# The opening stage of a pooled-attention and feed-forward kernel: keys of batch 1 loaded and pooled earlier, units of the first projection in another order

## The chip, the core and the metric

The kernel runs on one core of a Trainium2 chip. The metric is the time of one execution on the device in microseconds (us). TensorE (PE) multiplies, VectorE (DVE) and ScalarE (ACT) read its results out of PSUM, GpSimd (POOL) works between buffers in SBUF and also issues loads through its own software queue, and SyncE (SP) issues loads, stores and transposing transfers through a hardware queue. Each engine runs its instructions in the order of the program and waits on semaphores for the others.

## The reference, cut to what matters

```python
q, k, v: (8, 8, 576, 64) float32          # batch, heads, sequence, head size
k_p = k.reshape(B, H, 72, 8, D).mean(axis=3)   # 8 neighbouring keys become one
v_p = v.reshape(B, H, 72, 8, D).mean(axis=3)
scores = q @ k_p.T / sqrt(D);  attn = softmax(scores)
x = (attn @ v_p) as (4608, 512)
h = x @ w_in                               # w_in  512 x 2048
g = h - tanh(h)
out = g @ w_out                            # w_out 2048 x 512
```

## The kernel before, in words

Each of the 8 batches gives 512 queries to a group of its own (g = 0 to 7), in four blocks of 128 queries (j = 0 to 3). The 64 queries left over in each batch, its tail, are collected in pairs of batches and form a ninth group. For a group the kernel computes scores, softmax and attention for each block, turns the result x into xT, multiplies it with w_in (w1b in SBUF) to h, forms g = h - tanh(h) in gT, and multiplies with w_out (w2b). While one group is in its two large products, the attention of the next group is slipped in between.

The order of all work is written out by hand, and each engine gets its instructions in that order. PSUM has eight banks of 512 columns, and each use of a bank names its number.

The change lies in the opening stage, group 0, where nothing can be slipped under large products yet. These parts are touched:

* **Loads on the queue of POOL.** `load_w1(c)` (L187) brings the quarter c of w_in, the four quarters of hidden units, and casts it to bf16 on the way; `load_w2(c)` (L192) does so for w_out. `load_rows` (L131 and L137, two transfers) brings keys or values of a batch, `load_q` (L141) its queries. The order on this queue is: values of batch 0, w1 quarters 0, 1, 2, keys of batch 1, w1 quarter 3, queries of batch 1, w2 quarter 0, values of batch 1, w2 quarters 1 and 2, and later, behind other work of POOL, w2 quarter 3, queries of batch 2 and the tail of batches 0 and 1 (`tail_pieces`, L171).
* **Pooling keys.** `pool_k(1, nc.gpsimd)` adds eight keys to one in three additions on POOL (L209, L212, L215) and leaves them in kd. PE turns kd in five small products (`k_turn_pe`, recorded under L273), and DVE places the result in KB (L247).
* **Casting and turning queries.** `q_cast` (L261) makes bf16 from float32, one block each; `q_turn_pe` lets PE turn a block in four small products and ACT copy it into qT (L670).
* **h units.** `h_mm_quad(c, j, bank)` (L446) computes a quarter c of the hidden units, four times 128, for the block j: 16 products into one bank. It needs w1's quarter c and xT of the block j. `h_act_quads(c, j, bank)` (L472 tanh on ACT, L473 subtraction on DVE) empties two banks that hold the quarter c of the blocks j and j + 1. `h_tanh_quad` (L458) and `h_sub_quad` (L462) empty a single bank. xT of the blocks 2 and 3 comes last: `x_turn_pe` turns it on PE, and ACT copies it (L418).

There are 16 units (c, j). Behind them stands the second product of group 0, in 16 steps `o_unit0(u)` of four products each (L483): steps 0 to 3 use w2's quarter 0, steps 4 to 7 its quarter 1, and so on. Between these steps stand the scores (`s_unit`, L292 on PE, L304 and L307 on DVE), exponentials and values of batch 1. Step 1 releases the keys of batch 2, issued by SP (L131, L137); DVE pools them behind step 10, and SP turns them.

The tile framework gives the transfers of each kind of queue eight semaphores in rotation, so an issue waits until the transfer eight before it in the same rotation has landed.

Of the kernel before, what the change touches and what calls it, by code (L numbers as in the profile page):

```python
# [8 lines left out]
FP32 = mybir.dt.float32  # L9
BF16 = mybir.dt.bfloat16  # L10
ACT = mybir.ActivationFunctionType
# [9 lines left out]
R = 4  # L21
# [4 lines left out]
TG = 512  # L26
# [12 lines left out]
def kernel(  # L39
# [9 lines left out]
    nc = tc.nc  # L49
# [5 lines left out]
    tpool = ctx.enter_context(tc.tile_pool(name="tpool", bufs=3))  # L55
    psum = ctx.enter_context(tc.tile_pool(name="psum", bufs=1, space=PSUM))
    PS = psum.tile([128, 8, 512], FP32, name="PS")
    ctx.enter_context(tc.manual_schedule())

    def flat(b0, n):  # L60
        return PS[:, b0 : b0 + 2, :].rearrange("p k c -> p (k c)")[:, 0:n]
# [14 lines left out]
    gT = const.tile([128, NHID, TG], BF16, name="gT")  # L76
# [5 lines left out]
    q_raw = [const.tile([128, H, R, D], FP32, name=f"q_raw{i}") for i in range(2)]  # L82
# [42 lines left out]
    def load_rows(src, dst, b, t0=0, t1=NT, eng=None):  # L125
        eng = eng or nc.sync
        r = []
        n1 = min(t1, 4)
        if t0 < n1:
            r.append(  # L130
                eng.dma_start(  # L131
                    out=dst[:, t0:n1, :],
                    in_=src[b, 128 * t0 : 128 * n1, :].rearrange("(t p) n -> p t n", p=128),
                )
            )
        if t1 == NT:
            r.append(eng.dma_start(out=dst[0:64, 4, :], in_=src[b, 512:NK, :]))  # L137
        return r

    def load_q(b, dst, j0=0, j1=R, eng=None):  # L140
        return (eng or nc.sync).dma_start(  # L141
            out=dst[:, :, j0:j1, :],
            in_=q[b, :, 0:QA, :].rearrange("h (p j) d -> p h j d", j=R)[:, :, j0:j1, :],
        )
# [5 lines left out]
    def k_pieces(b):  # L150
        return row_pieces(k_rows, k_raw, b)
# [13 lines left out]
    def run(pieces, n=16):  # L165
        for _ in range(min(n, len(pieces))):
            pieces.pop(0)()

    def tail_pieces(i, eng=None):
        return [  # L170
            lambda s=s: (eng or nc.sync).dma_start(  # L171
                out=tl_raw[64 * s : 64 * s + 64, :, :],
                in_=q[2 * i + s, :, QA:S, :].rearrange("h p d -> p h d"),
            )
            for s in range(2)
        ]
# [9 lines left out]
    def load_w1(c):  # L186
        return nc.gpsimd.dma_start(  # L187
            out=w1b[:, :, c * 512 : (c + 1) * 512], in_=w1_src[:, :, c * 512 : (c + 1) * 512]
        )

    def load_w2(c):
        return nc.gpsimd.dma_start(  # L192
            out=w2b[:, c * 4 : (c + 1) * 4, :], in_=w2_src[:, c * 4 : (c + 1) * 4, :]
        )
# [10 lines left out]
    def pool_k(b, eng, t0=0, t1=NT):  # L205
        r = k_raw[b % 2].rearrange("p t (j d) -> p t j d", d=D)[:, t0:t1, :, :]
        kd = kds[b % 2][:, t0:t1, :, :]
        n = t1 - t0
        eng.tensor_tensor(  # L209
            out=r[:, :, 0:4, :], in0=r[:, :, 0:4, :], in1=r[:, :, 4:8, :], op=ALU.add  # L210
        )
        eng.tensor_tensor(  # L212
            out=r[:, :, 0:2, :], in0=r[:, :, 0:2, :], in1=r[:, :, 2:4, :], op=ALU.add
        )
        return eng.tensor_tensor(  # L215
            out=kd,
            in0=r[:, :, 0:1, :].to_broadcast([128, n, 2, D]),
            in1=r[:, :, 1:2, :].to_broadcast([128, n, 2, D]),
            op=ALU.add,
        )  # L220
# [39 lines left out]
    def q_cast(b, eng, j0=0, j1=R):  # L260
        eng(  # L261
            out=q_bf[b % 2][:, j0:j1, :, :].rearrange("p j h d -> p h j d"),
            in_=q_raw[b % 2][:, :, j0:j1, :],
        )
# [177 lines left out]
    def h_mm_quad(c, j, bank):  # L442

        for n in range(4):
            for fb in range(NFB):
                mm = nc.tensor.matmul(  # L446
                    PS[:, bank, 128 * n : 128 * n + 128],
                    lhsT=w1b[:, fb, (4 * c + n) * 128 : (4 * c + n + 1) * 128],
                    rhs=xT_of(0)[:, j, fb, :],
                    start=(fb == 0),  # L450
                    stop=(fb == NFB - 1),
                    skip_group_check=True,
                )
        return mm

    def h_tanh_quad(bank):
        t_sb = tpool.tile([128, 2, TG], FP32, name="t_sb2", tag="t_sb2")[:, 0, :]
        nc.scalar.activation(out=t_sb, in_=PS[:, bank, :], func=ACT.Tanh)  # L458
        return t_sb

    def h_sub_quad(c, j, bank, t_sb):
        nc.vector.tensor_sub(  # L462
            out=gT[:, 4 * c : 4 * c + 4, 128 * j : 128 * j + 128],
            in0=PS[:, bank, :].rearrange("p (n c) -> p n c", n=4),
            in1=t_sb.rearrange("p (n c) -> p n c", n=4),
        )

    def h_act_quads(c, j, bank):

        ps = PS[:, bank : bank + 2, :]  # L470
        t_sb = tpool.tile([128, 2, TG], FP32, name="t_sb2", tag="t_sb2")
        nc.scalar.activation(out=t_sb[:, :, :], in_=ps, func=ACT.Tanh)  # L472
        nc.vector.tensor_sub(  # L473
            out=gT[:, 4 * c : 4 * c + 4, 128 * j : 128 * j + 256].rearrange(
                "p n (j c) -> p j n c", j=2
            ),
            in0=ps.rearrange("p j (n c) -> p j n c", n=4),
            in1=t_sb.rearrange("p j (n c) -> p j n c", n=4),
        )
# [141 lines left out]
    ve, se, ge = nc.vector.tensor_copy, nc.scalar.copy, nc.gpsimd.tensor_copy  # L621
# [19 lines left out]
    for base, sign in ((G, 1), (-1, -1)):  # L641
        nc.gpsimd.affine_select(
            out=mask[:, :, :, 0],
# [20 lines left out]
    def q_turn_pe(b, j, bank, eng):  # L664
        for m in range(NHP):
            turn(
                PS[:, bank, m * 128 : (m + 1) * 128],
                q_bf[b % 2][:, j, 2 * m : 2 * m + 2, :].rearrange("p h d -> p (h d)"),
            )
        eng(out=qTs[b][:, j, :, :].rearrange("p m c -> p (m c)"), in_=PS[:, bank, :])  # L670
# [19 lines left out]
    w1_dmas.append(load_w1(1))  # L690
    for j in range(2, 4):
        q_cast(0, ge, j, j + 1)
    w1_dmas.append(load_w1(2))
    after(w1_dmas[1:], pooled)
    load_rows(k_rows, k_raw[1], 1, eng=nc.gpsimd)
    load_w1(3)
    load_q(1, q_raw[1], eng=nc.gpsimd)
    load_w2(0)
    load_rows(v_rows, v_bf[1], 1, eng=nc.gpsimd)
    load_w2(1)  # L700
    load_w2(2)
    kps = flat(4, NT * 128)
    k_turn_pe(0, 0, 2, kps)
    fill(1, 7)
# [48 lines left out]
    normalise((0, 1), x0[3])  # L753
    h_sub_quad(0, 1, 6, h_tanh_quad(6))
    h_sub_quad(1, 1, 7, h_tanh_quad(7))
    h_mm_quad(2, 0, 4)
    h_mm_quad(2, 1, 5)
    x_turn_pe(x0[3], 0, 3, 3, se)
    h_act_quads(2, 0, 4)
    pool_k(1, nc.gpsimd)  # L760
    load_w2(3)
    for j in range(R):
        q_cast(1, ge, j, j + 1)
    load_q(2, q_raw[0], eng=nc.gpsimd)
    run(tail_pieces(0, nc.gpsimd))
    h_mm_quad(0, 2, 6)
    h_mm_quad(0, 3, 7)
    h_act_quads(0, 2, 6)
    h_mm_quad(1, 2, 2)
    h_mm_quad(1, 3, 3)  # L770
    h_act_quads(1, 2, 2)
    h_mm_quad(2, 2, 4)
    kps = flat(0, NT * 128)
    k_turn_pe(1, 0, NT, kps)
# [1 line left out]
    h_mm_quad(2, 3, 5)  # L776
    h_act_quads(2, 2, 4)
    h_mm_quad(3, 0, 6)
    q_turn_pe(1, 0, 0, se)
    h_mm_quad(3, 1, 7)  # L780
    h_act_quads(3, 0, 6)
    q_turn_pe(1, 1, 1, se)
    h_mm_quad(3, 2, 2)
    h_sub_quad(3, 2, 2, h_tanh_quad(2))
    q_turn_pe(1, 2, 0, se)
    h_mm_quad(3, 3, 3)
    h_sub_quad(3, 3, 3, h_tanh_quad(3))
    q_turn_pe(1, 3, 1, se)

    def load_for(g):  # L790
# [41 lines left out]
    for u in range(16):  # L832
        mm = o_unit0(u)
        if u == 1:
            after(load_rows(k_rows, k_raw[0], 2, 0, 2), mm)
            run(k_pieces(2)[1:])
        if u == 0:
            exp_unit(0, s_unit(0, PA))
        if u == 1:
            exp_unit(1, s_unit(1, PB))  # L840
        if u == 2:
            sh2 = s_unit(2, PA)
        if u == 3:
            v_unit(2)
            exp_unit(2, sh2)
        if u == 4:
            e_turn_pe(slot(4), 0, se)
            exp_unit(3, s_unit(3, PB))
        if u == 5:
            e_turn_pe(slot(5), 0, se)  # L850
        if u == 6:
            e_turn_pe(slot(6), 2, se)
        if u == 7:
            a_unit(0, PA)
            e_turn_pe(slot(7), 2, se)
        if u == 8:
            a_unit(1, PA)
            x_turn_dma(x1[0], 1, 0, 2)
        if u == 9:
            a_unit(2, PB)  # L860
        if u == 10:
            a_unit(3, PA)
            x_turn_dma(x1[1], 1, 2, 2)
            for t in range(0, NT, 2):
                pool_k(2, nc.vector, t, min(t + 2, NT))
            q_turn_dma(2)
            k_turn_dma(2)
            k_place_kT(2, ge)
            run(v_pieces(2))
            turn_tail(0)  # L870
            load_for(1)
        if u >= 12:
            o_store(0, u % 4, OB[u % 4], (se, ve)[u % 2])
# [208 lines left out]
```

## Time and profile before

| | |
|---|---|
| median of 3 runs | 300.4 us (300.05 to 300.6) |
| the profiled execution, whole | 301.8 us |
| its span, first to last instruction | 300.1 us |
| mean granted TensorE clock | 0.991 |
| busy share of the span: PE, DVE, ACT, POOL | 95%, 69%, 48%, 41% |
| chain that ended last, by engine: PE, DVE, DMA | 77%, 8%, 7% |

The sums of the prediction are made against the profiled execution, which is 1.4 us above the median of the runs. In the rows of a timeline the first number is the start in us from the start of the span, the second the time in which the group of instructions was busy; brackets at the end give how long the engine sat idle before it, and what released it. A row "DMA to landing" gives smallest, median and largest time from the issue of a transfer to its landing. In the rows of a table by stretches each engine has its busy time and, in brackets, its instructions; PEclk is the granted clock of TensorE.

### The profile page before, as it was taken

The numbers are of one execution on the slowest core, as the hardware profiler recorded it, in microseconds if no ns is written. First come the engines' busy times: TensorE is split into PE (matmuls) and PEld (weight loads), VectorE is DVE, ScalarE is ACT, GpSimd is POOL, SyncE is SP. The second block draws the span as 40 slices with busy tenths as digits, with TensorE's granted clock in tenths as the row PEclk, the third lists the DMA queues.
The fourth block names the chain that finished last, engine by engine and source line by source line (L and its number), as shares of the span: only waits on it lengthen the run. The fifth ranks groups of instructions, "written<-read, shape, count | busy, mean of one in ns | idle before, by whom it ended". The sixth has DMA issues, their size and how long they took to land.

```text
span 300.1 us, 5150 instructions
## 1 busy us (share of the span) xinstructions
PE 286.5 (95%) x2011; PEld 167.5 (56%) x2027; DVE 206.2 (69%) x292; ACT 142.9 (48%) x200; POOL 121.7 (41%) x111
## 2 busy tenths in 40 slices
PE   6799799999999999999999999999999999999993
PEld 2489765444554455445544554455447854784582
DVE  6786484878835993398339932986699947945772
ACT  1786255158504851476137623672376345505620
POOL 7846906029610791098107910791063830010000
PEclk9999799999999999999999999999999999999998
DMA  7999996699988999886889798959823540011005
GB/s 233 225 283 272 205 264 172 129 262 314 228 219 212 332 151 217 239 298 114 204 248 312 137 185 257 328 73 214 232 68 69 103 167 17 2 70 73 0 3 140
DMA packets 84377, 54.55 MB, mean 182 GB/s; under 512 B 58976, under 2 KB 72416, under 8 KB 84352
## 3 DMA queue, kind: packets, MB, share of 16 engines
q1 hardware_dynamic: 77552, 44.90, 57.8%
q0 software_dynamic: 6416, 8.91, 14.3%
q10 hardware_dynamic: 384, 0.39, 0.5%
q8 instruction: 16, 0.26, 0.4%
q14 instruction: 9, 0.07, 0.1%
HBM read 36.70 MB, written 9.44 MB: 154 GB/s over the span
## 4 chain that ended last, share of the span: by engine, by line
PE 77%; DVE 8%; DMA 7%; POOL 3%; ACT 2%; issue 1%; SPq 0%; ACTq 0%; POOLq 0%; DVEq 0%
PE PS L426 32%; PE PS L483 26%; PE PS L561 11%; DMA k_raw<-in_k_dram 4%; PE PS L379 4%; DVE gT L440 3%; DMA q_raw<-in_q_dram 3%; PE PS L292 2%; DVE sh L307 2%; DVE mx L304 2%; PE PS L446 1%; POOL k_raw L209 1%; ACT t_sb L439 1%; PE PS L273 1%; POOL k_raw L212 1%
## 5 line engine op out<-in xcount | busy, mean ns | idle before, releaser
L440 DVE TENSOR_TENSOR gT<-PS,t_sb 128x1024 bf16<-128x1024 f32 x64 | 77.0, 1219 | 40.2 <-ACT t_sb L439 40.2
L426 PE MATMUL PS<-xT,w1b 128*128 128x512 bf16 x448 | 100.8, 379 | 0.0
L483 PE MATMUL PS<-w2b,gT 128*128 128x512 bf16 x368 | 88.7, 379 | 0.8
L439 ACT ACTIVATE t_sb<-PS 128x1024 f32<-128x1024 f32 x64 | 65.5, 1024 | 48.4 <-PE PS L426 47.0
L426 PEld LDWEIGHTS <-w1b 128*128 128x128 bf16 x512 | 49.4, 98 | 55.8
L483 PEld LDWEIGHTS <-gT 128*128 128x128 bf16 x384 | 35.3, 98 | 36.8
L505 ACT COPY o_h<-PS 128x512 f32<-128x512 f32 x22 | 12.8, 583 | 47.7 <-PE PS L483 44.0
L224 POOL TENSOR_TENSOR v_raw<-v_raw 128x1280 f32<-128x1280 f32 x6 | 17.4, 2908 | 35.7 <-DMA v_raw<-in_v_dram 35.7
L343 ACT ACTIVATE E<-sh 128x576 bf16<-128x576 f32 x31 | 21.2, 682 | 15.9 <-DVE sh L307 15.9
L307 DVE TENSOR_TENSOR sh<-PS,mx 128x576 f32<-128x576 f32 x35 | 26.5, 757 | 1.2
L304 DVE TENSOR_REDUCE mx<-PS 128x8 f32<-128x576 f32 x35 | 26.2, 748 | 1.5 <-PE PS L292 1.5
L400 DVE RECIPROCAL rden<-PS 128x8 f32<-128x8 f32 x36 | 7.4, 205 | 25.4 <-PE PS L379 23.4
L401 DVE TENSOR_TENSOR x_sb<-PS,rden 128x512 bf16<-128x512 f32 x32 | 22.1, 692 | 1.1
L561 PEld LDWEIGHTS <-q_raw 128*128 128x128 bf16 x192 | 18.5, 98 | 2.9 <-DVE q_raw L543 0.4
L247 POOL COPY KB<-kT 64x288 bf16<-64x288 bf16 x12 | 5.1, 421 | 35.6 <-DMA kT<-kd 30.2
L209 POOL TENSOR_TENSOR k_raw<-k_raw 128x1280 f32<-128x1280 f32 x6 | 17.4, 2908 | 0.0
L446 PE MATMUL PS<-xT,w1b 128*128 128x128 bf16 x256 | 17.2, 230 | 0.0
L446 PEld LDWEIGHTS <-w1b 128*128 128x128 bf16 x256 | 16.2, 104 | 0.0
L379 PEld LDWEIGHTS <-ET 128*128 128x128 bf16 x192 | 13.1, 98 | 5.2 <-ACT ET L362 0.8
L379 PE MATMUL PS<-VB,ET 128*128 128x130 bf16 (+2 forms) x192 | 15.8, 221 | 0.1
L561 PEld LDWEIGHTS <-gT 128*128 128x128 bf16 x144 | 13.9, 98 | 2.0
L292 PEld LDWEIGHTS <-qT 128*128 128x128 bf16 x128 | 10.0, 98 | 7.6 <-issue 0.8
(99 smaller groups left out, 290.7 us busy)
## 6 DMA issues: line engine op xcount, KB each, us to landing
k_raw<-in_k_dram SPq DMA_DIRECT2D x14, 512.0 KB, 8.6
q_raw<-in_q_dram SPq DMA_DIRECT2D x12, 512.0 KB, 6.9
v_raw<-in_v_dram SPq DMA_DIRECT2D x12, 512.0 KB, 5.1
out_dram<-o_h SPq DMA_DIRECT2D x24, 256.0 KB, 2.5
w1b<-in_moe_w_in_dram POOLq DMA_DIRECT2D x4, 512.0 KB, 9.0
q_raw<-in_q_dram POOLq DMA_DIRECT2D x2, 1024.0 KB, 14.2
w2b<-in_moe_w_out_dram POOLq DMA_DIRECT2D x4, 512.0 KB, 16.4
out_dram<-o_h SPq DMA_DIRECT2D x4, 512.0 KB, 3.3
```

The source lines that it names most:

```text
L209: eng.tensor_tensor(out=r[:, :, 0:4, :], in0=r[:, :, 0:4, :], in1=r[:, :, 4:8, :], op=ALU.add)
L304: nc.vector.reduce_max(out=mx.rearrange("p k h o -> p k (h o)"), in_=sc, axis=AX.X)
L307: nc.vector.tensor_tensor(out=sh[:, :, :, :], in0=sc, in1=mx.to_broadcast([128, 2, 4, G]), op=ALU.subtract)
L343: nc.scalar.activation(out=E[:, e, :, :].rearrange("p t c -> p (t c)")[:, 0:NK], in_=sh.rearrange("p k h c -> p (k h c)"), func=ACT.Exp, s ...
L379: nc.tensor.matmul(PS[ps, banks[half], D1 * h : D1 * (h + s1 - s0)], lhsT=ET[:, t, c0 : c0 + (ps.stop - ps.start)], rhs=VB[kb][:, t, s0:s1 ...
L401: nc.vector.tensor_tensor(out=x_sb, in0=ps[:, :, :, 0:D], in1=rden.to_broadcast([128, 2, 4, D]), op=ALU.mult,)
L426: nc.tensor.matmul(PS[:, bank, :].rearrange("p (j c) -> p j c", j=R), lhsT=w1b[:, fb, i * 128 : (i + 1) * 128], rhs=xT_of(g)[:, :, fb, :], ...
L439: nc.scalar.activation(out=t_sb[:, :, :], in_=ps, func=ACT.Tanh)
L440: nc.vector.tensor_sub(out=gT[:, i : i + 2, :], in0=ps, in1=t_sb[:, :, :])
L446: mm = nc.tensor.matmul(PS[:, bank, 128 * n : 128 * n + 128], lhsT=w1b[:, fb, (4 * c + n) * 128 : (4 * c + n + 1) * 128], rhs=xT_of(0)[:, ...
L483: mm = nc.tensor.matmul(PS[:, bank, 0 : c1 - c0], lhsT=gT[:, i, tb * 128 : (tb + 1) * 128], rhs=w2b[:, i, c0:c1], start=(i == 0), stop=(i ...
L561: nc.tensor.matmul(ps, lhsT=A[:, i, 128 * b : 128 * b + 128], rhs=B_[:, i, :], start=(n in "24" and i == 0), stop=(i == NQ - 1), skip_grou ...
```

## The change

On the queue of POOL the keys of batch 1 move ahead of w1's quarter 2. `pool_k(1)` moves from behind the first h units to the place ahead of the issues of w2's quarters 1 to 3; the casts of the queries of batch 1, w2's quarter 3 and the queries of batch 2 follow there in a row. The tail of batches 0 and 1 is no longer issued by POOL but by SP, at step 1 of the second product, behind the keys of batch 2. The h units come in another order: the blocks 2 and 3 of the quarters 0 and 1 first, then quarter 2. The units of one block and two quarters are emptied together by the new `h_act_quads2`. The turns of the queries of batch 1 stand one h unit later each, and the last two stand together.

```diff
+    def h_act_quads2(c, j, bank):
+        ps = PS[:, bank : bank + 2, :]
+        t_sb = tpool.tile([128, 2, TG], FP32, name="t_sb2", tag="t_sb2")
+        nc.scalar.activation(out=t_sb[:, :, :], in_=ps, func=ACT.Tanh)
+        nc.vector.tensor_sub(
+            out=gT[:, 4 * c : 4 * c + 8, 128 * j : 128 * j + 128],
+            in0=ps.rearrange("p k (n c) -> p (k n) c", n=4),
+            in1=t_sb.rearrange("p k (n c) -> p (k n) c", n=4),
+        )
...
     w1_dmas.append(load_w1(1))
     for j in range(2, 4):
         q_cast(0, ge, j, j + 1)
-    w1_dmas.append(load_w1(2))
     after(w1_dmas[1:], pooled)
     load_rows(k_rows, k_raw[1], 1, eng=nc.gpsimd)
+    load_w1(2)
     load_w1(3)
     load_q(1, q_raw[1], eng=nc.gpsimd)
     load_w2(0)
     load_rows(v_rows, v_bf[1], 1, eng=nc.gpsimd)
+    pool_k(1, nc.gpsimd)
     load_w2(1)
     load_w2(2)
+    for j in range(R):
+        q_cast(1, ge, j, j + 1)
+    load_w2(3)
+    load_q(2, q_raw[0], eng=nc.gpsimd)
...
-    h_mm_quad(2, 0, 4)
-    h_mm_quad(2, 1, 5)
+    h_mm_quad(0, 2, 4)
     x_turn_pe(x0[3], 0, 3, 3, se)
-    h_act_quads(2, 0, 4)
-    pool_k(1, nc.gpsimd)
-    load_w2(3)
-    for j in range(R):
-        q_cast(1, ge, j, j + 1)
-    load_q(2, q_raw[0], eng=nc.gpsimd)
-    run(tail_pieces(0, nc.gpsimd))
-    h_mm_quad(0, 2, 6)
-    h_mm_quad(0, 3, 7)
-    h_act_quads(0, 2, 6)
-    h_mm_quad(1, 2, 2)
-    h_mm_quad(1, 3, 3)
-    h_act_quads(1, 2, 2)
+    h_mm_quad(1, 2, 5)
+    h_act_quads2(0, 2, 4)
+    h_mm_quad(0, 3, 6)
+    h_mm_quad(1, 3, 7)
+    h_act_quads2(0, 3, 6)
+    h_mm_quad(2, 0, 2)
+    h_mm_quad(2, 1, 3)
+    h_act_quads(2, 0, 2)
     h_mm_quad(2, 2, 4)
     kps = flat(0, NT * 128)
     k_turn_pe(1, 0, NT, kps)
     k_place(1, kps[:, 0:NK], (ve, ve))
     h_mm_quad(2, 3, 5)
     h_act_quads(2, 2, 4)
     h_mm_quad(3, 0, 6)
-    q_turn_pe(1, 0, 0, se)
     h_mm_quad(3, 1, 7)
     h_act_quads(3, 0, 6)
-    q_turn_pe(1, 1, 1, se)
+    q_turn_pe(1, 0, 0, se)
     h_mm_quad(3, 2, 2)
     h_sub_quad(3, 2, 2, h_tanh_quad(2))
-    q_turn_pe(1, 2, 0, se)
+    q_turn_pe(1, 1, 1, se)
     h_mm_quad(3, 3, 3)
     h_sub_quad(3, 3, 3, h_tanh_quad(3))
+    q_turn_pe(1, 2, 0, se)
     q_turn_pe(1, 3, 1, se)
...
         if u == 1:
             after(load_rows(k_rows, k_raw[0], 2, 0, 2), mm)
             run(k_pieces(2)[1:])
+            run(tail_pieces(0))
```

## The prediction

> **What bounds the kernel now.** I read the page first, for the engine that fills the span and for places where it doesn't.
>
> ```profile
> span 300.1 us, 5150 instructions
> PE 286.5 (95%) x2011; PEld 167.5 (56%) x2027; DVE 206.2 (69%) x292; ACT 142.9 (48%) x200; POOL 121.7 (41%) x111
> PEclk9999799999999999999999999999999999999998
> ```
>
> PE is busy for 95%, so time is won only where PE stands still or runs slowly. The clock row shows one such place: the fifth slice (30.0 to 37.5 us). The table by stretches of 2 us shows it closer.
>
> ```profile
> 30.00:32.00 2.00, 0.01 (x1) 0.02 (x2) 1.23 (x1) 0.00 (x0) 1.92 (x3) 1.00 1.25 207
> 32.00:34.00 2.00, 2.00 (x20) 2.00 (x21) 0.91 (x2) 0.00 (x0) 2.00 (x4) 0.52 1.23 203
> 34.00:36.00 2.00, 2.00 (x26) 2.00 (x24) 0.56 (x1) 1.02 (x1) 2.00 (x4) 0.63 1.24 206
> ```
>
> The first engine column is PE: 0.01 us of work from 30 to 32 us, then granted clocks of 0.52 and 0.63. The chain of waits, cut to the first 64 us, names the cause.
>
> ```profile
> 12.24 12.50 DMA k_raw<-in_k_dram
> ...
> 25.03 0.74 POOL w2b L192
> ...
> 25.78 2.92 POOL k_raw L209
> ...
> 30.41 1.53 POOL kd L215
> 31.98 0.66 PE PS L273 x5
> 32.64 3.21 PE PS L446 x32
> ```
>
> The keys of batch 1 are issued at 12.24 and land at 24.74; POOL pools them from 25.78 until 31.94, 6.16 us; PE turns them at 31.98. PE's own timeline shows what it does around this.
>
> ```profile
> 23.13 1.95 PE L446 MATMUL PS<-xT,w1b 128*128 128x128 bf16 x32
> 24.91 0.39 PE L273 MATMUL PS<-ident,x_sb 128*128 128x128 bf16 x4
> 25.14 4.63 PE L446 MATMUL PS<-xT,w1b 128*128 128x128 bf16 x80
> 31.98 0.66 PE L273 MATMUL PS<-ident,kd 128*128 128x128 bf16 x5 [2.22 <-POOL kd L215]
> 32.43 3.42 PE L446 MATMUL PS<-xT,w1b 128*128 128x128 bf16 x32
> 35.69 0.39 PE L273 MATMUL PS<-ident,q_bf 128*128 128x128 bf16 x4
> ...
> 39.26 1.03 PE L483 MATMUL PS<-w2b,gT 128*128 128x512 bf16 x3
> ...
> 45.11 1.03 PE L483 MATMUL PS<-w2b,gT 128*128 128x512 bf16 x4
> ...
> 58.52 6.21 PE L426 MATMUL PS<-xT,w1b 128*128 128x512 bf16 x28
> ```
>
> At full clock 32 products take 24.91 - 23.13 = 1.78 us, 0.056 each, so a unit of 16 takes 0.89. The 80 products from 25.14 thus issue until 29.6: PE stands for 2.4 us. The next 32 take 35.69 - 32.43 = 3.26, which is 1.48 too long, and the five turns 0.45 for 0.28: another 0.17. **The stall costs 2.4, the low clock behind it 1.65, together 4.05 us.**
>
> **The change, part by part.** *Keys ahead of w1's quarter 2.* POOL's rows show when transfers land, since its issues wait for earlier ones.
>
> ```profile
> 18.24 0.54 POOL L137 DMA_DIRECT2D v_raw<-in_v_dram  x1 [1.52 <-DMA w1b<-in_moe_w_in_dram]
> 20.80 0.76 POOL L192 DMA_DIRECT2D w2b<-in_moe_w_out_dram  x1 [2.02 <-DMA w1b<-in_moe_w_in_dram]
> ...
> 31.87 0.78 POOL L192 DMA_DIRECT2D w2b<-in_moe_w_out_dram  x1
> 32.65 2.27 POOL L261 CAST q_bf<-q_raw 128x512 bf16<-128x512 f32 x4
> 34.87 0.90 POOL L141 DMA_DIRECT2D q_raw<-in_q_dram  x1
> 35.76 1.40 POOL L171 DMA_DIRECT2D tl_raw<-in_q_dram  x2
> ```
>
> POOL goes on 0.3 us after a landing (keys at 24.74, issue at 25.03). So w1's quarter 1 landed at about 18.0, quarter 2 at 20.5, 2.5 later, and the keys another 4.2 later. If the queue stays first in, first out, the keys land 2.5 (a quarter's time) to 4.2 us (their own) behind 18.0: at 20.5 to 22.2, and their fifth piece, issued 0.7 later, at most 0.4 behind. I take 22.5, by their own row. POOL starts 0.3 later, and kd is ready at 22.8 + 6.2 = 29.0 (bounds 27.0 and 29.1; before 31.94). The three transfers that swap have the same bytes, so w1's quarter 2 lands by 25.1 and its quarter 3 about when it did.
>
> *The order of the h units.* The timelines of ACT and DVE give what PE has to wait for.
>
> ```profile
> 22.97 0.58 ACT L418 CAST xT<-PS 128x512 bf16<-128x512 f32 x1 [0.42 <-PE PS L273]
> ...
> 28.97 1.02 ACT L472 ACTIVATE t_sb<-PS 128x1024 f32<-128x1024 f32 x1 [0.82 <-PE PS L446]
> ...
> 39.89 0.63 ACT L670 CAST qT<-PS 128x512 bf16<-128x512 f32 x1
> ```
>
> ```profile
> 26.88 2.52 DVE L473 TENSOR_TENSOR gT<-PS,t_sb 128x1024 bf16<-128x1024 f32 x2 [1.36 <-ACT t_sb L472]
> ...
> 32.57 0.94 DVE L247 CAST KB<-PS 64x288 bf16<-64x288 f32 x2 [1.32 <-PE PS L273]
> ...
> 55.25 0.68 DVE L209 TENSOR_TENSOR k_raw<-k_raw 128x512 f32<-128x512 f32 x1
> ```
>
> At 23.13 PE now wants xT of block 2 and finds it when ACT's copy ends, 22.97 + 0.58: a new wait of 0.4 us. From 23.5 it has 7 units (6.2) and a turn of x (0.2) before the turn of the keys, and comes to it at 29.95, where kd lies ready for 1.0 us (0.9 to 2.9 by the bounds). The 2.4 us go, and the low clock with them.
>
> Banks: a pair of units is emptied by 1.02 (tanh), 1.26 (subtraction, half of 2.52) and 0.3 for handovers (tanh at 28.97, behind products that end at 25.14 + 64 x 0.056 = 28.7), so 2.6 us behind its last product. By that the pairs are empty at 28.1, 29.9 and 31.6, and PE wants the banks again at 29.1, 31.1 and 33.1; w1's quarter 2 is wanted at 27.3, quarter 3 at 31.1. DVE places the keys behind the third subtraction, from 31.6 until 32.5, and the first turn of the queries wants that bank at 32.9: 0.4 to spare, the tightest cover; without it PE would wait one for one.
>
> *The turns of the queries.* The last ACT work ahead of the scores is four copies of about 0.5 and two single tanh of about 0.5 behind the pair's tanh. The pair ends on PE at 32.9, its tanh at 34.1, and the six run in a row until 37.15; before, the last copy ended at 39.89 + 0.63 = 40.5, and the scores of batch 1 wait for its bank. PE waits 0.3 for a bank ahead of the fourth turn, since two turns now stand together, and starts the second product at 35.9 instead of 39.26. Both differences are 3.35.
>
> **The sum:** -2.4 (stall) -1.65 (clock) +0.4 (xT of block 2) +0.3 (bank of the fourth turn) = -3.35 us at the scores of batch 1.
>
> *Loads behind the pooling.* w2's quarter 1 was issued at 20.80 and now waits for the pooling, until 29.0. Its landing, and that of the quarter issued at 31.87, by line:
>
> ```profile
> L192 POOL DMA_DIRECT2D w2b<-in_moe_w_out_dram x1: 764/764/764, 20.8 to 20.8; - x1
> ...
> DMA to landing us min/median/max: 17.2/17.2/17.2
> ```
>
> ```profile
> L192 POOL DMA_DIRECT2D w2b<-in_moe_w_out_dram x1: 780/780/780, 31.9 to 31.9; - x1
> ...
> DMA to landing us min/median/max: 11.3/11.3/11.3
> ```
>
> They landed at 38.0 and 43.2. The later issue landed faster, so it is the bytes ahead in the queue that set the landing, not the issue. Step 4 wants quarter 1 at 45.11 - 3.35 = 41.8. The bounds are 38.0 (bytes) and 29.0 + 17.2 = 46.2 (issue); by 29.0 + 11.3 it is 40.3. I take 38 to 40.3: cost 0, with the last 1.5 us as cover. Quarters 2 and 3 are wanted four and eight steps later. Quarter 3 and batch 2's queries stand behind two issues and the casts (2.27), which wait for the queries of batch 1; these had landed by 32.65. So they are issued between 32.8 and 35.8, against 31.87 and 34.87.
>
> *The tail by SP.* POOL loses 1.40 us of issuing that nothing waited for. SP's rows:
>
> ```profile
> 42.69 0.57 SPq L137 DMA_DIRECT2D k_raw<-in_k_dram  x1
> 52.92 3.67 SPq L409 DMA_TRANSPOSE xT<-x_sb  x2
> ```
>
> SP idles between these, so two issues of 0.7 fit. What matters is the data. The keys of batch 2 now are issued at 39.3 rather than 42.69, with batch 2's queries still in POOL's queue, and the tail behind them.
>
> ```profile
> DMA to landing us min/median/max: 9.7/9.7/9.7
> ```
>
> That row is the landing of the issue at 42.69: 52.4. DVE comes to pooling these keys at 55.25, 2.85 us later, and will come at 51.9. If they take 9.7 us again, they land at 49.0; if it is the sum of bytes that ends them, at 52.4, and DVE, PE's next supplier, is 0.5 late. The first transpose of x then comes at 49.6, with the tail perhaps still on its way. I take 0, bounds 0 and +1.5 (0.5 for the keys, 1.0 for a tail that holds up xT, which PE wants at 58.52 - 3.35).
>
> [...]
>
> From 58.5 us on, all of it hangs on events and moves along as a whole. So the profiled execution goes from 301.8 to 298.45, and the median, which stands 1.4 lower, **from 300.4 to 297.05 us**; I say 297.1.
>
> **Rivals.**
>
> *The low clock isn't the stall's.* The clock falls in the two stretches right behind the stall and, by the page, nowhere else but at the end. But it is one profiled execution: the timed runs may not have the dip. Then the gain is 2.4 - 0.7 = 1.7: 298.7. For it: the profiled execution stands 1.4 above the median, about the size of the dip. Against it: the dip begins where PE has stood still. [...] Chance 0.12.
>
> *The loads collide on the way into group 1* (above): 0.7 to 1.9 us given back, keys of batch 2 or x late: 298.2. For it: the share of the DMA engines is at its top (the 1.23 to 1.25 in the table). Against it: they are empty by 52.4 with the old order, and nothing is added. Chance 0.14.
>
> *The keys don't land earlier*, because the transfers of POOL's queue share the engines and not the order. Then kd comes at 24.74 + 0.4 + 0.3 + 6.2 = 31.6, PE stands 1.7 us from 29.95, with most of a dip: 300.2, no change. Against it: the issues above landed in order. Chance 0.03.
>
> *w2's quarter 1 is late: slower.* If its landing goes by its issue (17.2), PE waits at step 4 from 41.8 to 46.2: +4.4, net +1.05, 301.5. It turns from a gain into a loss if it lands later than 45.15, 16.1 us after issue; with a new dip behind the wait, 1.65 sooner. Against it: the 11.3 of the quarter issued at 31.87. Chance 0.07.
>
> **How the numbers follow.** The forecast holds 0.60, around 296.4 to 297.8: the key's early bound wins nothing, the new waits of 0.7 may be 0, copies and banks may cost 0.7 more. A gain beyond 4 us, under 296.4, has 0.04. The range, 296.4 to 299.0, takes in the collision and the lone stall and leaves out 0.14. Faster than 0.2% (0.6 us, what a measurement of this kernel can tell) are the forecast, the dip, the collision and the 0.04: 0.90; same 0.03; slower 0.07.
>
> **What would show it.** Right: in PE's timeline no wait on kd, PEclk at 1.00 from 24 to 40 us, the first L483 near 35.9, a wait of 0.4 ahead of the first unit of block 2, the pooling on POOL from 22.8. The first L426 x28 comes near 55.2. Wrong: PE waiting for w2b at step 4 near 42, DVE waiting for k_raw near 52, PE waiting for KB near 33, or a granted clock under 1 in another stretch.

## The result, and the profile after

The median went from 300.4 us to 298.27 us (8 executions, 297.96 to 299.4); the ratio to the kernel before is 0.9924, with a 95% interval of 0.9903 to 0.9945. That is 2.1 us, where 3.35 were forecast. The profiled execution took 298.33 us, against 301.8 before: 3.5 us less. The two differences don't agree, and most of what follows is about why.

The page of the kernel after, its first lines and its clock:

```profile
span 296.6 us, 5149 instructions
PE 284.8 (96%) x2011; PEld 166.0 (56%) x2027; DVE 206.2 (70%) x292; ACT 142.8 (48%) x200; POOL 120.3 (41%) x109
...
PEclk9999999999999999999999999999999999999998
```

The 7 in the fifth slice is gone. PE's timeline of the kernel after (start, busy time, and in brackets the idle time before and its releaser; L446 are h units, L273 turns, L494 is the second product, L483 before):

```profile
23.48 1.05 PE L446 MATMUL PS<-xT,w1b 128*128 128x128 bf16 x16 [0.32 <-ACT xT L418]
...
24.60 5.52 PE L446 MATMUL PS<-xT,w1b 128*128 128x128 bf16 x96
29.96 0.44 PE L273 MATMUL PS<-ident,kd 128*128 128x128 bf16 x5
30.23 2.84 PE L446 MATMUL PS<-xT,w1b 128*128 128x128 bf16 x48
...
35.15 0.88 PE L273 MATMUL PS<-ident,q_bf 128*128 128x128 bf16 x8
35.87 1.03 PE L494 MATMUL PS<-w2b,gT 128*128 128x512 bf16 x3
...
41.65 1.03 PE L494 MATMUL PS<-w2b,gT 128*128 128x512 bf16 x4
...
55.06 6.21 PE L426 MATMUL PS<-xT,w1b 128*128 128x512 bf16 x28
```

PE comes to the turn of the keys at 29.96 and does not wait. The second product starts at 35.87, 3.39 us before 39.26, and the first large product of group 1 at 55.06, 3.46 us before 58.52. POOL in the kernel after:

```profile
22.24 2.89 POOL L209 TENSOR_TENSOR k_raw<-k_raw 128x1280 f32<-128x1280 f32 x1 [3.58 <-DMA k_raw<-in_k_dram]
25.21 1.54 POOL L212 TENSOR_TENSOR k_raw<-k_raw 128x640 f32<-128x640 f32 x1
26.83 1.54 POOL L215 TENSOR_TENSOR kd<-k_raw 128x640 bf16<-128x640 f32 x1
28.32 1.53 POOL L192 DMA_DIRECT2D w2b<-in_moe_w_out_dram  x2
30.50 2.28 POOL L261 CAST q_bf<-q_raw 128x512 bf16<-128x512 f32 x4 [0.65 <-DMA q_raw<-in_q_dram]
32.72 0.74 POOL L192 DMA_DIRECT2D w2b<-in_moe_w_out_dram  x1
...
49.05 2.28 POOL L261 CAST q_bf<-q_raw 128x512 bf16<-128x512 f32 x4 [4.84 <-DMA q_raw<-in_q_dram]
51.28 0.61 POOL L179 CAST tl_bf<-tl_raw 128x512 bf16<-128x512 f32 x1
```

kd is ready at 26.83 + 1.54 = 28.37, 1.6 us before PE comes to it.

### The profile page after: what moved, and what is told of

Same layout as the page of the kernel before. It is cut to its first block, busy times and chain, and to the rows that moved or that the text cites. A ratio compares the mean times of both kernels' runs of the same rounds, so it can differ in the third digit from the quotient of the medians.

```text
span 296.6 us, 5149 instructions
## 1 busy us (share of the span) xinstructions
PE 284.8 (96%) x2011; PEld 166.0 (56%) x2027; DVE 206.2 (70%) x292; ACT 142.8 (48%) x200; POOL 120.3 (41%) x109
## 4 chain that ended last, share of the span: by engine, by line
PE 81%; DVE 10%; ACT 4%; DMA 1%; issue 1%; ACTq 0%; DVEq 0%
PE PS L426 32%; PE PS L494 26%; PE PS L572 11%; PE PS L379 4%; PE PS L446 4%; DVE gT L440 3%; PE PS L292 3%; DVE sh L307 2%; DVE mx L304 2%; DMA k_raw<-in_k_dram 1%; PE PS L273 1%; ACT ET L362 1%; ACT t_sb L439 1%; ACT E L343 1%; ACT E L327 1%
## 5 line engine op out<-in xcount | busy, mean ns | idle before, releaser
L494 PE MATMUL PS<-w2b,gT 128*128 128x512 bf16 x368 | 88.8, 379 | 0.8
L426 PEld LDWEIGHTS <-w1b 128*128 128x128 bf16 x512 | 49.4, 98 | 55.8
L494 PEld LDWEIGHTS <-gT 128*128 128x128 bf16 x384 | 35.3, 98 | 36.8
L446 PE MATMUL PS<-xT,w1b 128*128 128x128 bf16 x256 | 15.6, 219 | 0.3 <-ACT xT L418 0.3
L446 PEld LDWEIGHTS <-w1b 128*128 128x128 bf16 x256 | 14.7, 98 | 0.4 <-issue 0.4
```

Of the source, the lines that this page charges most:

```text
L426: nc.tensor.matmul(PS[:, bank, :].rearrange("p (j c) -> p j c", j=R), lhsT=w1b[:, fb, i * 128 : (i + 1) * 128], rhs=xT_of(g)[:, :, fb, :], ...
L446: mm = nc.tensor.matmul(PS[:, bank, 128 * n : 128 * n + 128], lhsT=w1b[:, fb, (4 * c + n) * 128 : (4 * c + n + 1) * 128], rhs=xT_of(0)[:, ...
L494: mm = nc.tensor.matmul(PS[:, bank, 0 : c1 - c0], lhsT=gT[:, i, tb * 128 : (tb + 1) * 128], rhs=w2b[:, i, c0:c1], start=(i == 0), stop=(i ...
```

## The experiments

The question was why the profiled execution won 3.5 us and the median only 2.1. Theory A: the stall and its low clock are there in every execution of the kernel before. Theory B: the low clock, 1.65 us, is there in some executions only, the profiled one among them. Beside that, each part of the change was tried alone or taken out. All times are medians, but for the two repeats of the kernel before, one execution each.

**Filling the stall.** PE gets zeros to multiply while it waits for the keys.

```diff
     kps = flat(0, NT * 128)
+    fill(10, 0)
     k_turn_pe(1, 0, NT, kps)
```

> The kernel before, with ten products of zeros (10 x 0.216 us at full clock) put on PE right ahead of the turn of the keys of batch 1, so that PE works through most of its 2.4 us stall; nothing else changes, and the keys are as late as before. Theory A, the low clock behind the stall is there in every execution: the filled kernel is 1.65 us faster than the one before also in the median, about 298.75. Theory B, the profiled execution of before had the dip but most timed executions do not, so that only the bare stall was won: the median moves by 0 to 0.5 us, 299.9 to 300.4. In both the profile shows the granted clock at 1.00 from 30 to 36 us and the turn of the keys still near 32.0.

Measured: 300.84 us in 12 executions, 299.77 to 301.34; the kernel before took 300.62 in 29 executions on that chip; the ratio is 0.998 (0.9958 to 1.0001). The median did not fall by 1.65, nor by the 1.0 that would be left of it after the 0.6 us that the fill cost in the profile below, so theory A falls. The spread says more than the median. The 29 executions of before lie in two groups, 18 of 299.98 to 300.81 and 11 of 301.48 to 302.78; of the 12 with the stall filled, none lies in the upper group. The groups are told by their times: the mean granted clock, 0.991 to 0.999 in the lower and 0.987 to 0.994 in the upper, does not part them alone, since a low clock at other places, as early on in the filled kernel below or behind the last product (0.58 from 298 to 300 us in the first profile), counts in it too. Of the 8 executions of before beside the result, one took 302.2 and one 301.15, between the groups. PE in the profile of the filled kernel:

```profile
9.62 1.07 PE L273 MATMUL PS<-ident,q_bf 128*128 128x128 bf16 x8 [0.65 <-ACT q_bf L261]
...
25.96 4.63 PE L446 MATMUL PS<-xT,w1b 128*128 128x128 bf16 x80
30.42 2.32 PE L616 MATMUL PS<-zeros 128*128 128x512 bf16 x10
32.58 0.44 PE L273 MATMUL PS<-ident,kd 128*128 128x128 bf16 x5
32.86 1.95 PE L446 MATMUL PS<-xT,w1b 128*128 128x128 bf16 x32
```

The 32 products behind the turn now issue in 34.65 - 32.86 = 1.79 us (the next row starts at 34.65), at full clock. The turn was expected near 32.0 and came at 32.58: in this execution PE reached the place 0.8 us late (25.96 against 25.14 in the first profile), and the zeros held it beyond the keys, which POOL had ready at 31.98. So the fill itself cost 0.6 us here; how often it does is not shown. PE was 0.4 us late already at 9.62, behind a wait for ACT (9.19 in the first profile); the rest came where the clock was low, by the table of stretches (PE's busy time is the first, PEclk the third number from the end):

```profile
8.00:10.00 2.00, 0.71 (x7) 0.34 (x6) 1.51 (x4) 1.05 (x2) 1.08 (x2) 1.00 1.24 267
10.00:12.00 2.00, 1.86 (x14) 1.27 (x14) 0.61 (x1) 1.22 (x3) 1.24 (x3) 0.56 1.23 202
12.00:14.00 2.00, 2.00 (x16) 1.47 (x14) 1.85 (x5) 1.30 (x7) 2.00 (x4) 0.59 1.24 207
```

**The kernel before, twice more**, unchanged.

> The kernel before, unchanged, for a second profile of it. Theory, the clock drops in only some executions: with chance 0.6 the profiled execution lies under 301, has no low clock between 25 and 40 us, and the second product begins near 37.6 to 37.9 instead of 39.26; with chance 0.4 it looks like the first profile. Rival, that the low clock is always there: it begins near 39.3.

> The kernel before, unchanged, a third profile, with the same two expectations.

Measured: 301.79 and 299.76 us; one more execution of before on that chip, timed only, took 301.57. The first looks like the first profile; the second has the same stall and no low clock. The turn of the keys on PE in the first, then PE in the second:

```profile
31.90 0.72 PE L273 MATMUL PS<-ident,kd 128*128 128x128 bf16 x5 [2.37 <-POOL kd L215]
```

```profile
24.90 4.63 PE L446 MATMUL PS<-xT,w1b 128*128 128x128 bf16 x80
31.95 0.45 PE L273 MATMUL PS<-ident,kd 128*128 128x128 bf16 x5 [2.42 <-POOL kd L215]
32.24 1.95 PE L446 MATMUL PS<-xT,w1b 128*128 128x128 bf16 x32
34.03 0.39 PE L273 MATMUL PS<-ident,q_bf 128*128 128x128 bf16 x4
...
37.60 1.03 PE L483 MATMUL PS<-w2b,gT 128*128 128x512 bf16 x4
```

The stretches of 2 us, of the first repeat and then of the second:

```profile
30.00:32.00 2.00, 0.10 (x2) 0.11 (x3) 1.02 (x1) 0.00 (x0) 1.92 (x3) 0.90 1.24 205
32.00:34.00 2.00, 2.00 (x20) 2.00 (x20) 0.91 (x2) 0.00 (x0) 2.00 (x4) 0.50 1.24 204
34.00:36.00 2.00, 2.00 (x30) 2.00 (x28) 0.59 (x1) 1.15 (x2) 2.00 (x4) 0.74 1.24 205
```

```profile
30.00:32.00 2.00, 0.05 (x1) 0.05 (x2) 1.01 (x1) 0.00 (x0) 1.92 (x3) 1.00 1.24 206
32.00:34.00 2.00, 2.00 (x37) 2.00 (x38) 0.91 (x2) 0.67 (x1) 2.00 (x4) 1.00 1.24 205
34.00:36.00 2.00, 2.00 (x40) 2.00 (x38) 1.22 (x1) 1.54 (x3) 2.00 (x4) 1.00 1.24 205
```

The same wait, 2.37 us in the one and 2.42 us in the other, was followed by a low clock in the one and not in the other. Without the low clock the second product starts at 37.60, 1.66 us before the 39.26 of the first profile, and the change takes it to 35.87: 1.73 us.

**The stall halved, and doubled.** Half as many zeros on PE; and, in a kernel of its own, work on POOL that holds the keys back.

```diff
+    fill(5, 0)
     k_turn_pe(1, 0, NT, kps)
...
+    nc.gpsimd.memset(xTt[:, :, :, :], 0.0)
+    nc.gpsimd.memset(o_hs[0][:, 0, :], 0.0)
     pool_k(1, nc.gpsimd)
     load_w2(3)
```

> The kernel before, with five products of zeros (1.08 us) on PE ahead of the turn of the keys, so that PE stands for about 1.3 us in place of 2.4; the keys are as late as before. The 29 executions of the kernel before fell into two groups, 18 of 299.98 to 300.81 us and 11 of 301.48 to 302.78, 1.6 us apart. Theory: the upper group is the executions in which the stall drops the clock, and half the stall is too short for that: all or nearly all executions at 300.0 to 300.9, median 300.4, none or one above 301.4. Rival: any stall at this place can drop the clock, and again 3 to 5 of 12 executions lie 1 to 1.6 us above the rest.

> The kernel before, with two clearings of buffers (about 2.6 us, of tiles that nothing has written yet) on POOL ahead of the pooling, so that the keys come 2.6 us later and PE stands for about 5 us. [...] Rival, that the low clock comes by chance and not by the length of the stall: median 303.0, with a third of the executions near 304.6.

Measured: with the stall halved 300.23 us (12 executions, 299.9 to 300.63), ratio 0.9973 (0.9952 to 0.9994). All twelve lie in the lower group, while 7 of the 17 executions of before on that chip lay at 301.79 to 302.46. The wait was 1.48 us in the profile. With the stall doubled 305.29 us, ratio 1.0118 (1.0087 to 1.015), all six executions between 303.93 and 305.81, none of them near 303.0. That is 0.7 more than the 304.6 that the 2.6 us and one low clock of 1.6 give on top of 300.4, and its stretches show why. The row of PE for the halved stall, then the stretches of the doubled one:

```profile
32.19 0.45 PE L273 MATMUL PS<-ident,kd 128*128 128x128 bf16 x5 [1.48 <-POOL kd L215]
```

```profile
30.00:32.00 2.00, 0.00 (x0) 0.00 (x0) 1.23 (x1) 0.22 (x1) 1.92 (x2) 1.00 1.23 206
32.00:34.00 2.00, 0.00 (x0) 0.00 (x0) 0.00 (x0) 0.00 (x0) 1.92 (x2) 0.61 1.24 204
34.00:36.00 2.00, 1.25 (x12) 1.25 (x13) 0.57 (x2) 0.00 (x0) 2.00 (x4) 0.50 1.24 206
36.00:38.00 2.00, 2.00 (x22) 2.00 (x20) 0.34 (x1) 0.79 (x1) 2.00 (x5) 0.50 1.25 209
38.00:40.00 2.00, 2.00 (x28) 2.00 (x26) 1.23 (x1) 0.82 (x2) 1.96 (x4) 0.68 1.24 205
```

The lowest stretches read 0.50; with that as half speed, a stretch of 2 us with clock c was low for 4 x (1 - c) us. Summed, the clock was low for 1.56 + 2 + 2 + 1.28 = 6.8 us here, against 0.4 + 2 + 1.04 = 3.4 in the first repeat above and 1.92 + 1.48 = 3.4 in the prediction's table. Of the 6.8 us, 4.5 lie behind the start of the keys' turn at 34.76, and at half speed they cost about 2.3 us, 0.7 more than the 1.6 counted on. Two of the six executions, 303.93 and 304.36, have a mean granted clock of 0.991, the other four 0.986 to 0.988; by that the clock was low for a shorter time in these two, which is argued from their times, since only one of the six was profiled.

The length of the stall alone does not tell whether the clock falls. In the profiles it was low at waits for the keys of 2.22 (first profile), 2.34 (units alone, below), 2.37 (first repeat) and 4.76 us, and stayed at 1.00 at 1.48 (halved) and 2.42 us (second repeat). Why two stalls as alike as 2.37 and 2.42 us differ is not shown. Counted by their times, the low clock came in 18 of the 46 executions of before on these two chips, 0.39, with a 95% interval of about 0.26 to 0.54.

**The loads alone, and the units alone.** The first has the new order of loads and the pooling, the old order of units and turns; the second has the new order of units and turns with the old order of loads and the pooling behind the issues of w2's quarters 1 and 2. The tail is issued by POOL in both. The edit of the first, cut:

```diff
-    w1_dmas.append(load_w1(2))
     after(w1_dmas[1:], pooled)
     load_rows(k_rows, k_raw[1], 1, eng=nc.gpsimd)
+    load_w1(2)
...
+    pool_k(1, nc.gpsimd)
     load_w2(1)
     load_w2(2)
```

> The new order of loads and pooling with the old order of h units, turns and the tail on the queue of POOL. Theory: kd is ready near 28.4 as after the change, but the unit (2, 0) stands first, at 23.1, and w1's quarter 2 now lands near 24.2, so PE waits 1.2 us there in place of the 2.4 at the keys. The median then is 0.8 us above that of the whole change, near 299.1. Rival, that the order of the h units is worth nothing: as fast as the whole change, 298.3.

> The new order of h units and turns with the old order of loads, the pooling behind the issues of w2 and the tail on the queue of POOL. Theory: PE comes to the turn of the keys at 29.95 and waits until 32.0 as before, 2.0 us, with a chance of the low clock behind it; the new order alone wins nothing: 300.4 (300.0 to 300.8). Rival, that emptying one block and two quarters together or the new order wins by itself: under 299.6.

Measured: loads alone 299.84 us, ratio 0.9965 (0.9943 to 0.9988). The stall moved rather than going away:

```profile
25.07 1.96 PE L446 MATMUL PS<-xT,w1b 128*128 128x128 bf16 x32 [1.40 <-DMA w1b<-in_moe_w_in_dram]
...
31.56 0.44 PE L273 MATMUL PS<-ident,kd 128*128 128x128 bf16 x5
31.84 1.95 PE L446 MATMUL PS<-xT,w1b 128*128 128x128 bf16 x32
34.11 0.38 PE L273 MATMUL PS<-ident,q_bf 128*128 128x128 bf16 x4 [0.32 <-DVE KB L247]
```

The wait for w1's quarter 2 took 1.40 where 1.2 were expected, and a wait of 0.32 for the bank of the keys came on top, which I had not expected. The kernel is 1.6 us behind the whole change, not 0.8 (across two chips). Units alone took 300.8 us, ratio 1.0004 (0.9981 to 1.0028), with a wait of 2.34 for the keys and 3 of 12 executions above 302: no gain, as expected. Its row of the keys' turn, and the stretch in which its clock fell, with a mean of 0.63:

```profile
32.84 0.72 PE L273 MATMUL PS<-ident,kd 128*128 128x128 bf16 x5 [2.34 <-POOL kd L215]
```

```profile
32.00:34.00 2.00, 1.16 (x12) 1.16 (x13) 0.48 (x2) 0.00 (x0) 2.00 (x3) 0.63 1.24 205
```

Loads alone won 0.8 us on their chip and units alone nothing, so neither half gives the whole gain; the order of units is what lets the later w1 quarter go unnoticed.

**The pooling behind the issues of w2, and the tail on POOL's queue.** Two kernels, each the whole change with one part undone.

```diff
-    pool_k(1, nc.gpsimd)
     load_w2(1)
     load_w2(2)
+    pool_k(1, nc.gpsimd)
+    load_w2(3)
     for j in range(R):
         q_cast(1, ge, j, j + 1)
-    load_w2(3)
...
     load_q(2, q_raw[0], eng=nc.gpsimd)
+    run(tail_pieces(0, nc.gpsimd))
...
             run(k_pieces(2)[1:])
-            run(tail_pieces(0))
```

> The whole change, but w2's quarters 1 and 2 are issued ahead of the pooling, as before the change. Theory: the second of these issues waits for the fifth piece of the keys, so that the pooling starts 0.8 to 1.5 us later and kd is ready at 29.2 to 29.9, still ahead of the turn at 29.96: the same time as the whole change, 298.3 within 0.3. Rival, that the pooling has to stand ahead of the issues: PE waits at the turn of the keys, 0.3 us or more slower.

> The whole change, but the tail of batches 0 and 1 is issued by POOL again, behind the queries of batch 2. Theory: nothing waits for the tail in either place, the same as the whole change, 298.3 within 0.3. Rival, that the tail behind the keys of batch 2 in SP's queue helps or harms: 0.5 us or more apart.

Measured: pooled behind the issues 298.53 us (298.2 to 298.92), ratio 0.9909 (0.9877 to 0.9941); the tail by POOL 298.23 us (297.92 to 299.34), ratio 0.9898 (0.9869 to 0.9927). Neither can be told from the whole change by its time. In the first, though, the profile shows the cover used up:

```profile
22.46 1.50 POOL L192 DMA_DIRECT2D w2b<-in_moe_w_out_dram  x2 [3.87 <-DMA k_raw<-in_k_dram]
23.97 2.93 POOL L209 TENSOR_TENSOR k_raw<-k_raw 128x1280 f32<-128x1280 f32 x1
26.98 1.54 POOL L212 TENSOR_TENSOR k_raw<-k_raw 128x640 f32<-128x640 f32 x1
28.59 1.54 POOL L215 TENSOR_TENSOR kd<-k_raw 128x640 bf16<-128x640 f32 x1
```

kd comes at 30.13, and PE, which reached the place at about 29.9, turns the keys at 30.19. That is 0.2 later than expected at the latest, and no longer ahead of the turn. So pooling first is worth up to 0.3 us in this profile, too little for the times to confirm.

**Two waits that the change left.** The change, with the fourth turn in another bank, and a quarter of a unit put where PE waited for xT of block 2.

```diff
-    def h_mm_quad(c, j, bank):
-        for n in range(4):
+    def h_mm_quad(c, j, bank, n0=0, n1=4):
+        for n in range(n0, n1):
...
-    h_mm_quad(1, 1, 7)
+    h_mm_quad(1, 1, 7, 0, 3)
     x_turn_pe(x0[2], 0, 2, 2, se)
     av_mms(slot(3), av_block(0), (0, 1))
+    h_mm_quad(1, 1, 7, 3, 4)
...
-    q_turn_pe(1, 3, 1, se)
+    q_turn_pe(1, 3, 7, se)
```

> The whole change and two edits. The last turn of the queries goes into bank 7 instead of bank 1, so that it need not wait for ACT's copy of the second (0.25 us), and the scores of batch 1 need not wait for the copy of the last (0.35 to 0.5 us). Four of the 16 products of the unit (1, 1) move behind the values of block 3, so that xT of block 2 is turned 0.2 us earlier and PE works while ACT copies it. Theory: the scores of batch 1 come 0.5 to 0.8 us earlier and all behind them: 297.6 (297.4 to 297.9) against 298.3. Rival, that DVE, which works until 36.8 at the last units, or the values on the way into group 1 set the time: no gain, 298.2 or more.

Measured: 297.62 us (297.38 to 298.3), ratio 0.9875 (0.9845 to 0.9905). The variant with the tail by POOL, which equals the change in time, took 298.23 on the same chip, 0.6 more; the intervals of the two ratios overlap, so this gain is likely, not certain. PE in its profile:

```profile
34.79 0.69 PE L273 MATMUL PS<-ident,q_bf 128*128 128x128 bf16 x8
35.31 1.03 PE L494 MATMUL PS<-w2b,gT 128*128 128x512 bf16 x4
36.26 0.41 PE L292 MATMUL PS<-KB,qT 128*128 128x144 bf16 x4
```

The second product starts at 35.31 instead of 35.87. It is the best of the kernels here.

## Why the prediction was right, and where it was off

The forecast was 297.1 us with a range of 296.4 to 299.0 and a chance of 0.90 for faster. 298.27 lies in the range and is faster, but the gain was 2.1 and not 3.35. It misses the forecast's own band, 296.4 to 297.8; the range holds it because it took in the first rival. By its steps:

* *Keys ahead of w1's quarter 2.* Right. POOL started at 22.24 (forecast 22.8) and kd was ready at 28.37 (29.0), inside its bounds. The issue of w1's quarter 2 at 12.71 landed 11.5 us later, at 24.2, and PE wanted it at 27.3.
* *The order of the h units.* Right. The new wait is 0.32 (forecast 0.4), the turn of the keys stands at 29.96 (29.95), the second product at 35.87 (35.9). The two turns that stand together took 0.72 (35.15 to 35.87), 0.2 more than with the fourth in another bank (34.79 to 35.31), where 0.3 of wait was forecast. The tightest cover, 0.4 for the bank of the keys, held; with the old order of units and the new loads it did not (0.32).
* *Loads behind the pooling.* Right. w2's quarter 1, issued at 28.32, landed 9.4 us later, at 37.7, and step 4 took it at 41.65. That the bytes ahead and not the issue set the landing is borne out: it was issued 7.5 us later and landed 0.3 earlier.
* *The tail by SP.* Right that it costs nothing. The keys of batch 2 landed 10.7 us behind the issue at 39.23, at 49.9, and DVE came to them at 51.80. What I had not seen is that batch 2's queries land later: POOL waited 4.84 us for them, until 49.05. The tail landed at 51.1, just ahead of its cast at 51.28; POOL's next work for PE, KB of batch 2, came at 58.56, waiting for SP's transpose, so nothing was behind it.
* *The sum for the profiled execution.* -3.35 forecast, -3.47 measured (301.8 to 298.33).
* *The step to the median* is the one that failed: the prediction put the same 3.35 under both, saying that the median "stands 1.4 lower". The term of 1.65 for the low clock was right in size (the medians of the two groups of the 29 executions are 300.48 and 302.04, 1.56 apart, and the second product of the first profile starts 1.66 later than that of the second repeat), but by their times it belongs to 18 of 46 executions, and the profiled one was among them. The median execution of before had the bare stall.

So the first rival, that the timed runs don't have the dip, describes the result; it stood at 0.12 and gave 298.7. Its own reason was half right: the low clock is the stall's, since filling or halving the stall removes it, but a stall of this length does not always bring it (2.42 us in the second repeat did not), and what else decides is not shown. That the time came out in the range thus owes more to this rival than to the sum. The hint was in the text as "for it": the profiled execution stood 1.4 above the median, about the size of the dip. It should have weighed more than the rest.

Some 0.2 to 0.4 us are left: the lone stall less the new waits gives 1.7, the profiles give 1.73, and the medians 2.1. On the two other chips the medians of the lower group, 300.48 and 300.22, lie 1.95 and 1.99 above the variants that equal the change in time (298.53 and 298.23). The turn of the keys came between 31.90 and 32.84 in the profiles with the old loads and no fill that overran (first profile 31.98, repeats 31.90 and 31.95, halved stall 32.19, units alone 32.84). The kernel before follows the landing of the keys one for one, and the kernel after has 1.6 us of cover for it. That would make before slower in the middle than in the profile without a dip, which at 299.76 lies at the lower end of its group. It is argued, not shown.

The slower rival (w2 late), the collision and the keys that land no earlier did not come true, by the landings above.

## What to carry to other kernels

A sum from one profiled execution has to be held against that execution's place among the timed ones: where it stands above the median by the size of one of the sum's terms, that term may be its own. The stall of TensorE here cost its length in every execution, and about 1.6 us more in those in which a low clock followed (18 of 46, by their times); shortening it to 1.5 us removed that part even before the stall was gone. Moving the load ahead paid in full only together with the order of the work: the load that gave way had to be wanted later.

## What the runs showed of the hardware that was not expected

The granted clock of TensorE was low, at 0.50, for 3.4 us at stalls of 2.22 and 2.37 us (first profile and first repeat) and, in the one profile of it, for 6.8 us at one of 4.76 us. At a stall of 2.42 us in another execution of the same kernel it stayed at 1.00. By the times, the same stall lowered it in 18 of 46 executions. It can also be low early: in the filled kernel's profile it was low from about 10.2 to 13.6 us, with means of 0.56 and 0.59 in two stretches, behind a stretch in which PE was busy for 0.71 of 2 us.
